# GateLoop attention and a PReLU MLP on one core: some of TensorE's waits are declared away

## The chip, the cores and the metric

The kernel runs on one NeuronCore of a Trainium2 chip. The metric is the device time of one execution in microseconds (us). Five engines work side by side, each through its own list of instructions in a fixed order: TensorE (PE in the profile: matmuls; PEld: its weight loads), VectorE (DVE), ScalarE (ACT), GpSimd (POOL) and SyncE (SP). SyncE does no arithmetic here; it issues all of the kernel's DMA transfers, one after the other. The engines meet through counters (semaphores): an instruction can be made to wait until another engine's counter, its own engine's counter or that of a DMA has reached a value.

## The reference

Two stages in float32. The first is a linear attention with a complex decay for each head and channel; the second is an MLP with a PReLU.

```python
# (batch, heads, seq, head_dim) = (4, 8, 768, 48)
mag = np.sqrt(a_re * a_re + a_im * a_im)
scale = np.minimum(mag, 0.999) / (mag + 1e-06)
a_re_n, a_im_n = (a_re * scale, a_im * scale)
for t in range(S):
    ar, ai = (a_re_n[:, :, t, :, None], a_im_n[:, :, t, :, None])
    new_re = ar * S_re - ai * S_im
    new_im = ar * S_im + ai * S_re
    kv = np.einsum('bhd,bhe->bhde', k[:, :, t], v[:, :, t])
    S_re, S_im = (new_re + kv, new_im)
    y[:, :, t] = np.einsum('bhd,bhde->bhe', q[:, :, t], S_re)
...
x = y.transpose(0, 2, 1, 3).reshape(3072, 384)
h = x @ w_in                                    # 384 -> 2048
g = np.maximum(h, 0.0) + alpha * np.minimum(h, 0.0)
return g @ w_out                                # 2048 -> 384
```

## The kernel before

The recurrence over 768 tokens is cut into 24 units: 4 batches by 6 chunks of 128 tokens (`unit(u)`). Before them, the `gates` tasks turn the gates into phases (`phs` in DRAM) and products of magnitudes (`decs` in DRAM) for several chunks at a time.

One unit works like this, with the names that the profile uses. SyncE loads `KQ` (queries and keys, three buffers), `PP` (phases, one buffer), `T` (products of decays, two buffers), `V` (values, **one** buffer) and `VL` (values laid out for six levels, one buffer, in some ten small transfers). VectorE multiplies `KQ` by the phases (L661, L663). Then come six levels h = 1, 2, 4, 8, 16, 32, taken two at a time in three visits. For a level, VectorE multiplies `KQ` by decays (L717), ScalarE copies the part that a product needs into `WQ` (L740; two slots that are handed around) or `W` (L756), TensorE multiplies keys by queries into a PSUM tile `ps_lv` (L678, two buffers), and VectorE (L702) or ScalarE (L699) masks the result into `A`. After the levels TensorE transposes the keys in two groups through one PSUM tile `ps_kt` (L785), and ScalarE copies each group into `T` (L787, L788). The product of keys and `V` goes to `ps_kv` (L797), one tile for each half (s = 0 and 1) of the chunk; VectorE decays the state `St` (L826) and adds `ps_kv` (L829), once for each half. The output `ps_y` is opened by four bf16 products (L808), gathers the products of `A` and `VL` (L817) and of `KQ` and `St` (L841), and is copied by ScalarE into `T` (L855) and sent to DRAM (`ysc`, L860).

For the MLP, `xT` is loaded back from `ysc` for one or two chunks (L873); TensorE computes `ps_h` (L889), ScalarE and VectorE make the PReLU (L896, L898), and TensorE sums `ps_o` (L908). There are 672 products on L889 and 384 on L908; in the trace a float32 product is two matmul records.

The order is written out by hand. Each task (gates, loads, units, MLP) is a Python generator; the string `ORDER` names, letter by letter, which task takes its next step. `A` to `I` are the gates, `J` the loads of `KQ`, `PP` and `T`, `K` the spreading of values in DRAM (L560), `L` the loads of `V` and `VL`, `M` to `O` the weights, `P` to `Z` and `a` to `m` the 24 units, `n` the loads of `xT`, and `o` the MLP. So the place of every instruction in its engine's list is fixed, that of every DMA in SyncE's list too. The waits are not written by hand: the framework derives them from the tiles that an instruction reads and writes. One wait can sit on the instruction itself; further ones stand ahead of it as instructions of their own (EVENT_SEMAPHORE in the trace). What is already implied by an earlier wait of the same engine is left out.

The lines around which the change turns are the loads of `V` in `loads_v` (L603, L605, L608), which are not edited:

```python
nc.sync.dma_start(V[0:P - 16], v[b, :, 1:P - 15, c].rearrange("n p e -> p n e"))       # L603
```

and the functions that are:

Of the kernel before, what the change touches and what calls it, by code (L numbers as in the profile page):

```python
# [9 lines left out]
F32 = mybir.dt.float32  # L10
# [3 lines left out]
AF = mybir.ActivationFunctionType  # L14
ALU = mybir.AluOpType
# [3 lines left out]
P = 128  # L19
# [82 lines left out]
def kernel(  # L102
# [32 lines left out]
    nc = tc.nc  # L135
    B, HP, _, D, S = q.shape
# [5 lines left out]
    D2 = 2 * D  # L142
    HC = P // 2
# [5 lines left out]
    VISITS = [(1, 2), (4, 8), (16, 32)]  # L149
    LEVELS = [h for visit in VISITS for h in visit]  # L150

    qv = q.rearrange("b n i d s -> b d (n i) s")
    kv_in = k.rearrange("b n i d s -> b d (n i) s")
# [2 lines left out]
    work = ctx.enter_context(tc.tile_pool(name="work", bufs=2))  # L156
    dram = ctx.enter_context(tc.tile_pool(name="dram", bufs=4, space=DRAM))
    ps = ctx.enter_context(tc.tile_pool(name="ps", bufs=1, space=PSUM))

    def halves(t, h):  # L160

# [3 lines left out]
    ident = consts.tile([P, P], F32, tag="ident")  # L165
# [20 lines left out]
    for h in (16, 32):  # L186
        by_row[h] = []
        for m in range(HC // h):
            t = next(column)
# [8 lines left out]
    def step(*args, **kwargs):  # L198
# [5 lines left out]
        KQ=3, PP=1, T=2, V=1, WQ=2, W=1, run=1, St=3, xT=2, raw0=1, raw1=1, raw2=1, g0=0, g1=0, g2=0, ot=2, top=2,  # L204
        lv=2, misc=1, y=1, h=2, o=1).items()}
# [255 lines left out]
    start = consts.tile([D2, B, H], F32, tag="start")  # L461
# [104 lines left out]
    def loads():  # L566
        for u in range(NU):
            b, c = divmod(u, NCH)
            cols = slice(c * P, (c + 1) * P)
            yield DMA(196, takes=(R["KQ"],))  # L570
            KQ = work.tile([D2, 2, H, P], F32, tag="KQ", name="KQ", bufs=3)
            n = min(P, S - 1 - c * P)
            if n < P:
                nc.gpsimd.memset(KQ[:, 1, :, n:P], 0.0)
            for i in range(2):
                rows = slice(i, D2, 2)
                if i:
                    yield DMA(196)
                nc.sync.dma_start(KQ[rows, 0], qv[b, :, :, cols])
                t = yield DMA(196)  # L580
                nc.sync.dma_start(KQ[rows, 1, :, 0:n], kv_in[b, :, :, c * P + 1:c * P + 1 + n])
            done["KQ", u] = t
            loaded[u] = L = dict(KQ=KQ)
            t = yield DMA(393, ("PP", u), takes=(R["PP"],))
            scr, phs, at = scr_of[u]
            L["PP"] = PP = work.tile([D2, H, P + 1], F32, tag="PP", name="PP", bufs=1)
            nc.sync.dma_start(PP, phs.rearrange("(h d) i s -> (d i) h s", d=D)[:, :, at * P:(at + 1) * P + 1])
            done["rotation", u] = t
            for i in range(2):
                rows = slice(i, D2, 2)  # L590
                t = yield DMA(393, ("T", u), takes=() if i else (R["T"],))
                if i == 0:
                    L["T"] = T = work.tile([P, H, TL], F32, tag="T", name="T", bufs=2)
                nc.sync.dma_start(T[rows], scr.rearrange("(h d) c s -> d h c s", d=D)[:, :, at])
            done["decays", u] = t

    def loads_v():
# [47 lines left out]
    def unit(u):  # L645
        b, c = divmod(u, NCH)
        r = yield DVE(H * P, ("KQ", u), ("rotation", u), takes=(R["WQ"],))
        L = loaded[u]
        KQ, PP = L["KQ"], L["PP"]
# [17 lines left out]
        def meet(h, shared, at, keys, queries, *after, takes=()):  # L667

            e = yield PE(0.28, *after, *[("met", h, u - 1)] * (u > 0), takes=takes, mode=1, n=16)
            if not shared:  # L670
                shared.append(ps.tile([P, 2, HP, HC // 2], F32, tag="lv", name="ps_lv", bufs=2))
            t = shared[0][:, at]
            for p in range(4):
                for i in range(2):
                    n = 4 * i + p
                    for g in range(2):
                        j = HC // 2 * g
                        nc.tensor.matmul(t[64 * i + j:64 * i + j + HC // 2, p], lhsT=keys(n, g),  # L678
                                         rhs=queries(n, g), start=True, stop=True)
            done["met", h, u] = e  # L680
            return e

        def mask_out(name, t, e):

            n = HC

            if name in by_row:
                e = yield ACT(HP * name + 100, e, takes=(R[name],))
            else:
                e = yield DVE(HP * n, e, takes=(R[name],))  # L690
            a = A[name] = work.tile([P, HP, n], F32, tag=f"A{name}", name=f"A{name}",
                                    bufs=2 if name <= 4 else 1)
            if name in by_row:
                for m, s in enumerate(by_row[name]):
                    if m:
                        e = yield ACT(HP * name + 100, e)
                    cols = slice(m * name, (m + 1) * name)
                    at = m * name % (HC // 2)
                    nc.scalar.activation(a[:, :, cols], t[:, :, at:at + name], AF.Copy, scale=s)  # L699
            else:  # L700
                whole = [P, HP, 2, HC // 2]
                nc.vector.tensor_tensor(out=a.rearrange("p n (g t) -> p n g t", g=2), in0=t.unsqueeze(2).to_broadcast(whole),  # L702
                                        in1=masks[name].rearrange("p (g t) -> p g t", g=2).unsqueeze(1).to_broadcast(whole),
                                        op=ALU.mult)
            made.append(e)
            return e

        def step(h, x0=None):

# [9 lines left out]
        if c == 0:  # L719
            k_ = yield DMA(144, *[("state", u - 2)] * (u > 1), takes=(R["St"],))  # L720
            St = work.tile([D2, H, D], F32, tag="St", name="St", bufs=3)
# [6 lines left out]
        for visit in VISITS:  # L728
            ready = []
            for h in visit:  # L730
                held, slot, w = None, None, k_
                if h == 1:
                    held, slot = "WQ", first_slot
                    keys, queries = [lambda n, g, z=WQ, i=i: z[:, i, n, HC // 2 * g:HC // 2 * (g + 1)] for i in (1, 0)]
                elif h != visit[-1]:
# [6 lines left out]
                    keys, queries = [lambda n, g, z=z, i=i: z[:, i, n, HC // 2 * g:HC // 2 * (g + 1)] for i in (1, 0)]  # L742
                else:
                    def queries(n, g, h=h):
                        m = HC // (2 * h)
                        return halves(KQ[:, 0, n], h)[:, :, 1][:, m * g:m * (g + 1)]

                    if h == HC // 2:
                        def keys(n, g):
                            return KQ[:, 1, n, P // 2 * g:P // 2 * g + HC // 2]  # L750
                    else:
# [6 lines left out]
                        keys = lambda n, g, W=W: W[:, n, HC // 2 * g:HC // 2 * (g + 1)]  # L758
                ready.append((h, keys, queries, held, slot, w))
                if h != visit[-1]:  # L760
                    k_ = yield DVE(2 * H * HC, w, *[("decays", u)] * (h == 1))
                    T = L["T"]
                    step(h, WQ if h == 1 else None)
            tiles, shared = [], []
# [8 lines left out]
                k_ = yield DVE(2 * H * HC, e)  # L773
                step(visit[-1])
            for h, ta, e in tiles:
                e = yield from mask_out(h, ta, e)
            R["lv"].put(e)
        q_ = k_

# [1 line left out]
        for i in range(2):  # L781
            e = yield PE(0.333, k_, takes=(R["misc"],), n=2)
            t = ps.tile([P, HP, D2], F32, tag="misc", name="ps_kt")
            for p in range(4):
                nc.tensor.transpose(t[:, p], KQ[:, 1, 4 * i + p], ident[:D2, :D2])  # L785
            e = yield ACT(HP * P + 80, e, ("decays", u))
            nc.scalar.copy(T[:, 4 * i:4 * (i + 1), 0:D2], t)  # L787
            nc.scalar.copy(T[:, 4 * i:4 * (i + 1), D2:P], t[:, :, 0:P - D2])  # L788
            R["misc"].put(e)
        e = yield PE(0.72, e, ("V", u), *[("state", u - 1)] * (u > 0), takes=(R["misc"],) if last else (R["misc"], R["lv"]), mode=2, n=16 if last else 32)  # L790
        V = L["V"]
# [1 line left out]
        for n in range(H):  # L793
            for j in range(0, P, HC):
                for s in range(1 if last else 2):
                    rows = slice(HC * s, HC * (s + 1))
                    nc.tensor.matmul(kv[s][j:j + HC, n], lhsT=T[rows, n, j:j + HC],  # L797
                                     rhs=V[rows, n // 2, (n % 2) * D:(n % 2 + 1) * D], start=True, stop=True)
        ek = e
        for s in range(2):  # L800
            for part in range(2):
# [20 lines left out]
        for s in range(1 if last else 2):  # L822
            before, known = states[s]
            k_ = yield DVE(H * D, known, takes=(R["St"],))
            St = work.tile([D2, H, D], F32, tag="St", name="St", bufs=3)
            nc.vector.tensor_tensor(out=St, in0=before, in1=T[0:D2, :, TL - 4 + s:TL - 3 + s].to_broadcast([D2, H, D]),  # L826
                                    op=ALU.mult)
            k_ = yield DVE(H * D, ek, k_)
            nc.vector.tensor_tensor(out=St, in0=St, in1=kv[s][0:D2], op=ALU.add)  # L829
            R["lv" if s else "misc"].put(k_)  # L830
            states.append((St, k_))
        if not last:
# [4 lines left out]
        for s in range(2):  # L837
            before, known = states[s]
            e = yield PE(0.47, q_, known, mode=1, n=8)
            for n in range(H):  # L840
                nc.tensor.matmul(Y[64 * (n % 2):64 * (n % 2) + D, n // 4, n // 2 % 2, HC * s:HC * (s + 1)],  # L841
                                 lhsT=before[:, n], rhs=KQ[:, 0, n, HC * s:HC * (s + 1)],
                                 start=False, stop=(s == 1 and n // 2 % 2 == 1))
            R["St"].put(e)
        R["KQ"].put(e)
        if g not in ysc_of:
# [154 lines left out]
```

## Time and profile before

| | |
|---|---|
| time before, median of 3 runs | 843.26 us (841.33 to 843.42) |
| span of the profiled execution | 845.2 us |
| TensorE busy | 699.6 us (83%) |
| VectorE busy | 653.3 us (77%) |
| ScalarE busy | 443.3 us (52%) |
| GpSimd busy | 196.3 us (23%) |
| packets of the DMA queue that SyncE feeds, as a share of 16 engines' span | 59.2% |

The profiled execution's own time is its span, 845.2 us from the first to the last instruction; it is 1.9 us (0.2%) above the median of the timed runs. In a line of the timeline the first number is the start in us from the beginning of the span, the second the length of the group, then the engine, the source line, the operation, what is written and what is read, the shape, and how many instructions are merged. Square brackets tell idle time of the engine ahead of it and what ended it. "SPq" is SyncE issuing a DMA, "PEldq" is TensorE's sequencer; a wait that is an instruction of its own is not counted as busy. The clock of TensorE that a throttle granted stands as a share of full speed.

### The profile page before, as it was taken

How to read it: one execution, taken by the hardware profiler on the slowest of the kernel's cores; microseconds unless marked ns; L12 is line 12 of the kernel's file. 1: busy time of each engine (PE TensorE's matmuls, PEld its weight loads, DVE VectorE, ACT ScalarE, POOL GpSimd, SP SyncE). 2: the span in 40 equal slices, each digit the busy share in tenths (PEclk: the TensorE clock that was granted, in tenths of full speed). 3: DMA queues.
4: the chain of work that ended last, by engine and by line, in shares of the span. 5: the costliest groups of instructions: out<-in, count | busy, mean ns of one | idle time of the engine just before them, and what ended most of it. 6: DMA issues, size and time to landing. Idle time of an engine off the chain costs nothing.

```text
span 845.2 us, 26866 instructions
## 1 busy us (share of the span) xinstructions
PE 699.6 (83%) x11488; PEld 529.6 (63%) x11488; DVE 653.3 (77%) x1020; ACT 443.3 (52%) x937; POOL 196.3 (23%) x293
## 2 busy tenths in 40 slices
PE   0002316688899999999999999999999999999998
PEld 0001315566777777767777777777676777777776
DVE  5999998689998999979998997687877656345212
ACT  7679686356745656665565634555444324233211
POOL 6241421126544411450115404300124000000000
PEclk9999997879999999999999999999999999999999
DMA  8496987675469677736965467747644482231100
GB/s 240 142 270 172 281 198 207 186 203 123 118 201 255 143 182 223 182 88 172 264 166 138 134 178 181 201 107 192 159 136 106 115 204 64 69 80 38 37 29 9
DMA packets 194174, 130.91 MB, mean 155 GB/s; under 512 B 74120, under 2 KB 185864, under 8 KB 194056
## 3 DMA queue, kind: packets, MB, share of 16 engines
q1 hardware_dynamic: 194056, 129.20, 59.2%
q8 instruction: 90, 1.47, 0.8%
q14 instruction: 28, 0.23, 0.1%
HBM read 100.82 MB, written 35.71 MB: 162 GB/s over the span
## 4 chain that ended last, share of the span: by engine, by line
PE 63%; DVE 17%; DMA 6%; issue 6%; ACT 5%; SPq 2%; POOL 0%; DVEq 0%; ACTq 0%; POOLq 0%
PE ps_o L908 25%; PE ps_h L889 25%; PE ps_lv L678 4%; DVE KQ L717 4%; PE ps_y L817 3%; PE ps_kv L797 2%; PE ps_y L841 2%; DVE gate L338 2%; DMA PP<-phs 2%; DMA phs<-gate 1%; DMA g_sb<-in_w_in_dram 1%; PE ps_kt L785 1%; DVE gate L426 1%; SPq L626 1%; DVE gate L340 1%
## 5 line engine op out<-in xcount | busy, mean ns | idle before, releaser
L889 PE MATMUL ps_h<-xT,w_in_sb 128*128 128x256 f32 (+1 forms) x1344 | 302.0, 356 | 2.9 <-DVE g_sb L898 1.6
L908 PE MATMUL ps_o<-w_out_sb,g_sb 128*128 128x384 f32 x768 | 295.2, 499 | 5.1 <-DVE g_sb L898 4.9
L889 PEld LDWEIGHTS ps_h<-xT,w_in_sb 128*128 128x128 f32 x1344 | 234.3, 193 | 74.1 <-issue 3.6
L898 DVE SCALAR_TENSOR_TENSOR g_sb<-g_sb,al,ps_h 128x256 f32<-128x256 f32 (+1 forms) x224 | 97.4, 437 | 115.5 <-ACT g_sb L896 115.1
L896 ACT ACTIVATE g_sb<-ps_h 128x256 f32<-128x256 f32 (+1 forms) x224 | 79.0, 353 | 204.2 <-PE ps_h L889 202.7
L908 PEld LDWEIGHTS ps_o<-w_out_sb,g_sb 128*128 128x128 f32 x768 | 138.0, 192 | 56.7 <-DVE g_sb L898 6.9
L717 DVE TENSOR_TENSOR KQ<-KQ,T 96x1024 f32<-96x1024 f32 x120 | 148.5, 1239 | 32.1 <-PE ps_lv L678 23.2
L678 PE MATMUL ps_lv<-WQ 96*32 96x32 f32 x2304 | 34.7, 204 | 79.0 <-DVE WQ L661 55.9
L678 PEld LDWEIGHTS ps_lv<-WQ 96*32 96x32 f32 x2304 | 26.6, 116 | 99.7 <-DVE WQ L661 56.1
L740 ACT COPY WQ<-KQ 96x1024 f32<-96x1024 f32 x48 | 50.0, 1041 | 27.8 <-DVE KQ L717 27.7
L338 POOL TENSOR_TENSOR gate<-gate 128x72 f32<-128x72 f32 x42 | 29.6, 704 | 125.6 <-ACT gate L368 122.8
L855 ACT COPY T<-ps_y 48x256 f32<-48x256 f32 x96 | 30.8, 364 | 51.8 <-PE ps_y L841 51.2
L338 DVE TENSOR_TENSOR gate<-gate 128x576 f32<-128x576 f32 (+5 forms) x84 | 50.0, 595 | 1.1
L515 POOL TENSOR_SCALAR top<-top 128x768 f32<-128x768 f32 x16 | 41.5, 2602 | 32.1 <-ACT top L507 32.1
L678 PE MATMUL ps_lv<-KQ,W 96*32 96x32 f32 x1536 | 25.2, 205 | 27.5 <-ACT W L756 23.2
L817 PE MATMUL ps_y<-A,VL 64*48 64x64 f32 x2304 | 42.4, 223 | 4.1 <-DMA VL<-vsc 2.5
L699 ACT ACTIVATE A<-ps_lv,columns 128x64 f32<-128x64 f32 x144 | 36.2, 336 | 17.2 <-PE ps_lv L678 17.1
L426 DVE TENSOR_TENSOR gate<-gate 128x1152 f32<-128x1152 f32 (+2 forms) x36 | 43.6, 1235 | 0.3
L756 ACT COPY W<-KQ 96x512 f32<-96x512 f32 x48 | 30.8, 642 | 23.9 <-DVE KQ L717 21.1
L817 PEld LDWEIGHTS ps_y<-A,VL 64*48 64x48 f32 x2304 | 39.8, 124 | 5.5 <-DMA VL<-vsc 2.7
L678 PEld LDWEIGHTS ps_lv<-KQ,W 96*32 96x32 f32 x1536 | 20.3, 115 | 29.6 <-ACT W L756 24.7
L785 PE MATMUL ps_kt<-ident,KQ 96*128 96x96 f32 x192 | 26.0, 260 | 15.4 <-DVE KQ L717 12.9
(106 smaller groups left out, 912.1 us busy)
## 6 DMA issues: line engine op xcount, KB each, us to landing
T<-decs SPq DMA_DIRECT2D x48, 384.0 KB
PP<-phs SPq DMA_DIRECT2D x24, 387.0 KB
KQ<-in_q_dram SPq DMA_DIRECT2D x48, 192.0 KB
decs<-gate SPq DMA_DIRECT2D x7, 1152.0 KB
phs<-gate SPq DMA_DIRECT2D x14, 576.0 KB
KQ<-in_k_dram SPq DMA_DIRECT2D x40, 192.0 KB
vsc<-in_v_dram SPq DMA_DIRECT2D x48, 144.0 KB
VL<-vsc SPq DMA_DIRECT2D x24, 288.0 KB
```

Source lines behind the costliest of these rows:

```text
L338: on(4 * k).tensor_tensor(out=m, in0=w[:, 1::-1].unsqueeze(2).to_broadcast([P, 2, 2, k]), in1=pairs_of(u), op=ALU.mult)
L426: TT(out=m[:, a], in0=U5[:, 1 + a], in1=turned(off3, o)[:, a].unsqueeze(1).unsqueeze(3).to_broadcast([P, L // 2, nb, 2]), op=ALU.mult)
L515: nc.gpsimd.tensor_scalar(out=top, in0=top, scalar1=F64_SMALL, scalar2=None, op0=ALU.max)
L678: nc.tensor.matmul(t[64 * i + j:64 * i + j + HC // 2, p], lhsT=keys(n, g), rhs=queries(n, g), start=True, stop=True)
L699: nc.scalar.activation(a[:, :, cols], t[:, :, at:at + name], AF.Copy, scale=s)
L717: nc.vector.tensor_tensor(out=x, in0=x if x0 is None else x0, in1=m, op=ALU.mult)
L740: nc.scalar.copy(z.rearrange("p i n t -> p i (n t)").rearrange("p i (m h) -> p m i h", h=h), bass.AP(tensor=KQ.tensor, offset=KQ.offset + ...
L817: nc.tensor.matmul(o, lhsT=Vp[h][64 * i:64 * i + 64, s, e_ * D:(e_ + 1) * D], rhs=a, start=False, stop=False)
L889: nc.tensor.matmul(p, lhsT=w_in_sb[:, f // 2, kk, f % 2 * P:(f % 2 + 1) * P], rhs=x_of[m][:, kk], start=(kk == 0), stop=(kk == NK - 1))
L896: nc.scalar.activation(gt, p, AF.Relu, scale=-1.0)
L898: nc.vector.scalar_tensor_tensor(out=gt, in0=gt, scalar=al_1[:, f:f + 1], in1=p, op0=ALU.mult, op1=ALU.add)
L908: nc.tensor.matmul(sums[0], lhsT=gt[:, c * P:(c + 1) * P], rhs=w_out_sb[:, f], start=(f == 0), stop=(f == NF - 1))
```

## The change

Three helpers are added. `of(group, i)` puts an instruction into a named group; `turned(i)` declares that an instruction need not wait for the members of the group `turned`; `read(group, i)` declares an instruction to be the fence of a group, that is, one by whose end all members of the group are done. Members of a group don't wait for one another.

- The loads into `KQ` and `T` (and the one small fill of `KQ`) become members of `turned`, and TensorE's products that read these tiles (L678, L785, L797, L841) are declared not to wait for them.
- The products of the second visit (levels 4 and 8) become members of a group `lv` of their unit, with the last mask of that visit as its fence.
- Each of the two groups of transposes (L785) becomes a group `kt`, with ScalarE's second copy (L788) as its fence.
- The products into each of the two `ps_kv` tiles (L797) become a group `kv`, with VectorE's addition to the state (L829) as its fence.

No instruction is added, removed or moved on any engine apart from the waits; tiles and buffers are the same.

```diff
+    def of(group, i):
+        tc.add_to_no_dep_group(group, i.ins)
+        return i
+    def read(group, i):
+        tc.declare_fence(i.ins, group=group)
+        return i
+    def turned(i):
+        tc.declare_no_dep(i.ins, group="turned", reason="the engine that this waits for overwrote all of it")
+        return i
...
-                nc.gpsimd.memset(KQ[:, 1, :, n:P], 0.0)
+                of("turned", nc.gpsimd.memset(KQ[:, 1, :, n:P], 0.0))
...
-                nc.sync.dma_start(KQ[rows, 0], qv[b, :, :, cols])
+                of("turned", nc.sync.dma_start(KQ[rows, 0], qv[b, :, :, cols]))
...
-                nc.sync.dma_start(KQ[rows, 1, :, 0:n], kv_in[b, :, :, c * P + 1:c * P + 1 + n])
+                of("turned", nc.sync.dma_start(KQ[rows, 1, :, 0:n], kv_in[b, :, :, c * P + 1:c * P + 1 + n]))
...
-                nc.sync.dma_start(T[rows], scr.rearrange("(h d) c s -> d h c s", d=D)[:, :, at])
+                of("turned", nc.sync.dma_start(T[rows], scr.rearrange("(h d) c s -> d h c s", d=D)[:, :, at]))
...
-                shared.append(ps.tile([P, 2, HP, HC // 2], F32, tag="lv", name="ps_lv", bufs=2))
+                shared.extend([ps.tile([P, 2, HP, HC // 2], F32, tag="lv", name="ps_lv", bufs=2), h])
...
-                        nc.tensor.matmul(t[64 * i + j:64 * i + j + HC // 2, p], lhsT=keys(n, g),
-                                         rhs=queries(n, g), start=True, stop=True)
+                        met = turned(nc.tensor.matmul(t[64 * i + j:64 * i + j + HC // 2, p], lhsT=keys(n, g),
+                                                      rhs=queries(n, g), start=True, stop=True))
+                        if shared[1] == VISITS[1][0]:
+                            of(f"lv {u}", met)
...
             for h, ta, e in tiles:
-                e = yield from mask_out(h, ta, e)
+                e, i = yield from mask_out(h, ta, e)
+            if visit == VISITS[1]:
+                read(f"lv {u}", i)
...
-                nc.tensor.transpose(t[:, p], KQ[:, 1, 4 * i + p], ident[:D2, :D2])
+                of(f"kt {u} {i}", turned(nc.tensor.transpose(t[:, p], KQ[:, 1, 4 * i + p], ident[:D2, :D2])))
...
-            nc.scalar.copy(T[:, 4 * i:4 * (i + 1), D2:P], t[:, :, 0:P - D2])
+            read(f"kt {u} {i}", nc.scalar.copy(T[:, 4 * i:4 * (i + 1), D2:P], t[:, :, 0:P - D2]))
...
-                    nc.tensor.matmul(kv[s][j:j + HC, n], lhsT=T[rows, n, j:j + HC],
-                                     rhs=V[rows, n // 2, (n % 2) * D:(n % 2 + 1) * D], start=True, stop=True)
+                    of(f"kv {u} {s}", turned(nc.tensor.matmul(
+                        kv[s][j:j + HC, n], lhsT=T[rows, n, j:j + HC],
+                        rhs=V[rows, n // 2, (n % 2) * D:(n % 2 + 1) * D], start=True, stop=True)))
...
-            nc.vector.tensor_tensor(out=St, in0=St, in1=kv[s][0:D2], op=ALU.add)
+            read(f"kv {u} {s}", nc.vector.tensor_tensor(out=St, in0=St, in1=kv[s][0:D2], op=ALU.add))
...
-                nc.tensor.matmul(Y[64 * (n % 2):64 * (n % 2) + D, n // 4, n // 2 % 2, HC * s:HC * (s + 1)],
-                                 lhsT=before[:, n], rhs=KQ[:, 0, n, HC * s:HC * (s + 1)],
-                                 start=False, stop=(s == 1 and n // 2 % 2 == 1))
+                turned(nc.tensor.matmul(Y[64 * (n % 2):64 * (n % 2) + D, n // 4, n // 2 % 2, HC * s:HC * (s + 1)],
+                                        lhsT=before[:, n], rhs=KQ[:, 0, n, HC * s:HC * (s + 1)],
+                                        start=False, stop=(s == 1 and n // 2 % 2 == 1)))
```

More of the change, by code (lines that the diff above doesn't have):

```diff
@@ L698, in mask_out @@
                     at = m * name % (HC // 2)
-                    nc.scalar.activation(a[:, :, cols], t[:, :, at:at + name], AF.Copy, scale=s)
+                    i = nc.scalar.activation(a[:, :, cols], t[:, :, at:at + name], AF.Copy, scale=s)
             else:
                 whole = [P, HP, 2, HC // 2]
-                nc.vector.tensor_tensor(out=a.rearrange("p n (g t) -> p n g t", g=2), in0=t.unsqueeze(2).to_broadcast(whole),
+                i = nc.vector.tensor_tensor(out=a.rearrange("p n (g t) -> p n g t", g=2), in0=t.unsqueeze(2).to_broadcast(whole),
                                         in1=masks[name].rearrange("p (g t) -> p g t", g=2).unsqueeze(1).to_broadcast(whole),
@@ L705, in mask_out @@
             made.append(e)
-            return e
+            return e, i
         def step(h, x0=None):
```

## The prediction

> **What bounds the kernel now.** I read the page first, then the stretches, TensorE's waits and the timeline around the loads of `V`.
>
> ```profile
> span 845.2 us, 26866 instructions
> PE 699.6 (83%) x11488; PEld 529.6 (63%) x11488; DVE 653.3 (77%) x1020; ACT 443.3 (52%) x937; POOL 196.3 (23%) x293
> PEclk9999997879999999999999999999999999999999
> ...
> 235.00:400.00 165.00, 162.62 (x2752) 123.26 (x2751) 151.90 (x204) 93.89 (x213) 55.65 (x81) 1.00 0.72 184
> 400.00:600.00 200.00, 196.90 (x3272) 147.14 (x3271) 169.28 (x228) 108.68 (x237) 43.15 (x82) 1.00 0.69 174
> ...
> PE ps_h L889 <- DVE g_sb L898: 1.6, 2, 0.8
> L797 PEldq EVENT_SEMAPHORE  x56: 51/51/1457, 82.3 to 788.5; - x56
> ```
>
> Until about 235 us TensorE has little to do; from there it is the bound (162.62 busy of 165, 196.90 of 200), and its idle time after 235 is 13.7 us in all four stretches to the end. So whatever makes TensorE wait after 235 us lengthens the kernel nearly one for one, and hardly anything is there to be gained.
>
> **The change, part by part.** The built programs have the same instructions in the same order; the waits differ.
>
> *Taken away.* Standalone waits on TensorE fall from 244 to 171. Each takes 51 ns in the sequencer (last line above). Both ends: 73 x 0.051 = 3.7 us saved, and 0. The sequencer works ahead of the array: the waits ahead of a product on L797 stand at 82 to 788 us one to four us before that product starts, and where one lasts long (up to 1457 ns, TensorE's own transposes) the product then still waits for ScalarE's copy (L788), which comes later. The cover is that copy; without it a bubble would be shorter by at most those waits. I take -0.5. TensorE also gets 35 new waits for itself, all for work 20 or more products back, over 5 us earlier: 0.
>
> *Moved, and this decides.* With the addition L829 declared the fence of the products L797, what must follow those products follows the addition instead. That holds for the next load of `V` (L603): in 21 of 24 units it waited for TensorE's L797 and now waits for VectorE's second L829. VectorE comes to that addition when its own list does: in 14 of the 21 units it ended later than the load was issued before, by 1.1 to 11.9 us, 68.6 us in all. And the load heads SyncE's one list: `VL`, `KQ`, `xT`, `PP`, `T`, `ysc` and the output stand behind it. Three places reach TensorE.
>
> ```profile
> 220.87 0.31 SPq L603 DMA_DIRECT2D V<-in_v_dram  x1
> 224.11 2.76 SPq L626 DMA_DIRECT2D VL<-in_v_dram  x3
> 226.92 0.59 SPq L873 DMA_DIRECT2D xT<-ysc  x1
> ...
> 222.65 0.54 DVE L829 TENSOR_TENSOR St<-St,ps_kv 96x384 f32<-96x384 f32 x1
> 232.19 0.54 DVE L829 TENSOR_TENSOR St<-St,ps_kv 96x384 f32<-96x384 f32 x1
> ...
> 235.95 1.46 PE L889 MATMUL ps_h<-xT,w_in_sb 128*128 128x256 f32 x6
> ```
>
> First: the addition ends at 232.73, so `V` goes from 220.87 to about 232.8, +11.9. SyncE idled 1.6 us (222.51 to 224.11) ahead of the `VL` loads, so `xT` is issued 11.9 - 1.6 = 10.3 later, at 237.2. Its last semaphore count came 4.95 us after its issue (the trace's semaphore record; `PP`, as large, took 5.8, from 582.26 to the product at 588.05 that waited for it). It lands at 242.2 and TensorE wanted it at 235.95: +6.2. SyncE's two long issues of small loads (1.28 and 1.44 us, others of their kind 0.5 to 0.6) may shrink when they come late: 4.6 is the low end, 7.0 the high one (additions late by 0.8 themselves). I take 6.2.
>
> ```profile
> 364.75 0.32 SPq L603 DMA_DIRECT2D V<-in_v_dram  x1
> 377.70 0.44 SPq L629 DMA_DIRECT2D VL<-vsc  x1
> ...
> 372.56 0.55 DVE L829 TENSOR_TENSOR St<-St,ps_kv 96x384 f32<-96x384 f32 x1
> 384.85 1.61 PE L817 MATMUL ps_y<-A,VL 64*48 64x64 f32 x96
> ```
>
> Second: +8.4, less 1.0 of SyncE's idle time on the way: `VL` is issued 7.4 later. It landed 4.2 us before the product that reads that part of it (semaphore record): +3.2, or 1.3 if two long issues shrink. Both load and product shift by the first stall, so this comes on top. I take 3.
>
> ```profile
> 650.86 0.31 SPq L603 DMA_DIRECT2D V<-in_v_dram  x1
> 661.92 0.81 SPq L629 DMA_DIRECT2D VL<-vsc  x1
> ...
> 661.70 0.54 DVE L829 TENSOR_TENSOR St<-St,ps_kv 96x384 f32<-96x384 f32 x1
> 674.84 1.53 PE L817 MATMUL ps_y<-A,VL 64*48 64x64 f32 x96
> ```
>
> Third: +11.4, less 0.7; 9.0 us of slack: +1.7 (0 to 1.7). Loads with 1 to 2 us of slack (`VL` at 447.6, `xT` at 324.0) add 1 (0 to 2). In the other units the slack covers the delay.
>
> *Added elsewhere.* Six copies `WQ` (L740) now wait for the last mask of the second visit (L702), 0.6 to 1.7 us later than they ran, 5.4 in all: +1.5, since TensorE waited for what follows in about half (0 to 5.4). VectorE gets 13 waits for itself on L717: an instruction that waits for its neighbour starts 0.03 us after its end, one that doesn't 0.08 before it (medians of the trace): 13 x 0.11 = 1.5 at most; +0.5, since VectorE is not the bound after 235. [...] ScalarE's copies on L855 wait for L829 too, in 33 places, 32 of them long done, one 0.3 us late at 95 us where TensorE idles: 0.
>
> *Given back.* TensorE's waits after 235 for engines that were not behind it: -2 (0 to -4).
>
> Sum: -0.5 + 6.2 + 3 + 1.7 + 1 + 1.5 + 0.5 - 2 = 11.4. Against its own execution that is 845.2 to 856.6 of span; against the median, 843.26 + 11.4 = 854.7.
>
> **Rivals.**
>
> (a) *The loads are hidden.* If SyncE catches up (short issues, shorter landings), the first stall shrinks to 1 or 2 and the others vanish, with ScalarE's 1.5 given back: 843.3 to 845.8. For it: most of the 14 delays die in slack. Against: 4.1 us of slack against 10.3. Somewhat less catching up gives 846 to 850.
>
> (b) *Faster.* One mechanism: TensorE's waits for its own transposes (L797, to 1457 ns) and for loads keep its sequencer from running ahead, and products after them start late. It decides if the copy L788 ends before those waits do. All idle time after 235 that could go is 13.7; the named wait on L797 would give a third of it: 838.5. Against it: what ended the waits there is ScalarE's copy, 7.6 us in 13 cases on that line's weight loads.
>
> (c) *The stall slows the clock too.*
>
> ```profile
> 170.07 1.65 PE L908 MATMUL ps_o<-w_out_sb,g_sb 128*128 128x384 f32 x2 [4.29 <-DVE g_sb L898]
> 169.30:176.00 6.70, 5.93 (x42) 4.60 (x43) 5.42 (x11) 3.69 (x5) 4.67 (x3) 0.50 1.03 294
> ```
>
> An idle stretch of 4.29 us stands ahead of 6.7 us at a granted clock of 0.50; two such products took 1.65 there and 0.91 at 189.5. After 190 the clock stayed at 1.00. A stall of 6.2 us at 236 may bring 3.4 to 10.2 us (the shortest and longest such stretch between 138 and 190) at half clock: 1.7 to 5.1 more, 856.4 to 860. [...]
>
> (d) *It doesn't do what it says*: the waits leave TensorE but its times stay, and the new waits on VectorE are met. Then 843.3, counted with (a).
>
> **How the numbers follow.** 0.3% (2.5 us) is about what a measurement of this kernel can tell from no change. Forecast, 850 to 856.4: 0.50. Clock as well: 0.18. Partly caught up, 846 to 850: 0.16. Hidden, within 0.3%: 0.09. Faster: 0.07. So slower 0.84, same 0.09, faster 0.07. The range leaves out the faster case and half of the hidden one below, 844.5; above, all high ends together (7.0 + 3.2 + 1.7 + 2 + 1.5 + 1.5 = 16.9, with 3 of clock) give 863.
>
> **What would show it.** The loads of `V` right behind L829 in SyncE's list; a wait of TensorE for `xT<-ysc` near 236 of 4.6 to 7 us, and for `VL<-vsc` near 391 and 686; the slice of the clock behind the first one. Wrong if no wait for `xT` appears there, or if TensorE's idle time after 235 falls below 13.7 us.

## The result, and the profile after

The changed kernel takes 862.02 us (median of 4 runs, 860.59 to 871.23); the kernel before took 842.48 us beside it (841.33 to 843.42). The medians lie 19.5 us apart, a quotient of 1.0232; the ratio that is estimated from all runs of both kernels is 1.0262, 95% interval 1.0216 to 1.0308. The profiled execution of the changed kernel is its fastest, 860.59 us, of which the span is 858.9 us. Between the two profiled executions the span grew by 13.7 us.

The head of the page after:

```profile
span 858.9 us, 26799 instructions
PE 704.3 (82%) x11488; PEld 532.6 (62%) x11488; DVE 654.0 (76%) x1020; ACT 442.3 (52%) x937; POOL 188.9 (22%) x293
```

The stretches behind 235 us (length, then busy us and instructions of TensorE, its weight loads, VectorE, ScalarE and GpSimd, then granted clock, DMA share, GB/s):

```profile
235.00:400.00 165.00, 154.40 (x2646) 116.32 (x2636) 143.80 (x196) 86.38 (x200) 51.57 (x83) 0.98 0.66 170
400.00:600.00 200.00, 195.10 (x3171) 145.70 (x3161) 169.46 (x227) 109.33 (x236) 44.85 (x81) 0.99 0.67 174
600.00:860.00 260.00, 253.48 (x3389) 189.90 (x3387) 135.08 (x214) 85.97 (x230) 17.86 (x39) 1.00 0.36 92
```

TensorE is busy 602.98 us after 235 us, so its idle time there is 858.9 - 235 - 602.98 = 20.9 us, 7.2 more than before. In both executions 3.5 us of the idle time lie behind TensorE's last product. Its busy time over the whole span grew by 4.7 us with the same instructions, and in the first 235 us it was busy for 1.8 us less. 7.2 + 4.7 + 1.8 = 13.7.

What ended TensorE's idle time after 236 us (us in all, times, longest), and what SyncE waited for ahead of the load of `V`, which is L618 now:

```profile
PE ps_y L837 <- DMA VL<-vsc: 5.6, 3, 2.3
PE ps_h L909 <- DMA xT<-ysc: 4.5, 2, 3.8
PE ps_lv L693 <- ACT W L773: 2.9, 3, 1.1
PE ps_y L837 <- issue: 2.0, 4, 1.0
...
SPq L618 <- DVE St L849: 82.4, 13, 15.8
SPq L618 <- DVE g_sb L918: 17.0, 3, 15.2
```

Neither of the first two stood in the list of before. SyncE's wait ahead of L603 was 34.7 us for TensorE; ahead of L618 it is 82.4 us for the addition L849 (L829 before). The 15.2 us that the last line puts down to `g_sb` are the wait ahead of 235.04 us, which the timeline shows to end with the addition too. Of the 24 loads of `V`, 15 are issued 0.03 us after an addition ends. The first place behind 235 us in the timeline after:

```profile
234.47 0.54 DVE L849 TENSOR_TENSOR St<-St,ps_kv 96x384 f32<-96x384 f32 x1
235.04 0.31 SPq L618 DMA_DIRECT2D V<-in_v_dram  x1
236.12 2.11 SPq L641 DMA_DIRECT2D VL<-in_v_dram  x3
238.27 0.60 SPq L893 DMA_DIRECT2D xT<-ysc  x1
...
242.17 2.93 PE L909 MATMUL ps_h<-xT,w_in_sb 128*128 128x256 f32 x6 [3.79 <-DMA xT<-ysc]
```

The load of `V` is issued 0.03 us after the second addition ends, `xT` stands behind it, and TensorE waits 3.79 us for it. Just ahead of this wait the same instructions ran 2.4 us later than before, from here on 6.2. Three further places, at each of which the last load of `VL` comes too late:

```profile
384.75 0.32 SPq L618 DMA_DIRECT2D V<-in_v_dram  x1
395.94 0.47 SPq L644 DMA_DIRECT2D VL<-vsc  x1
399.18 1.34 PE L837 MATMUL ps_y<-A,VL 64*48 64x64 f32 x80 [2.31 <-DMA VL<-vsc]
...
468.64 1.34 PE L837 MATMUL ps_y<-A,VL 64*48 64x64 f32 x80 [1.88 <-DMA VL<-vsc]
...
690.00 1.33 PE L837 MATMUL ps_y<-A,VL 64*48 64x64 f32 x80 [1.44 <-DMA VL<-vsc]
```

And the clock, in the stretches right behind the first wait and behind the one at 468 us (TensorE's busy time first, granted clock third from the end):

```profile
241.20:248.10 6.90, 5.93 (x74) 4.11 (x74) 1.75 (x2) 0.87 (x2) 0.46 (x2) 0.51 0.62 153
469.90:473.30 3.40, 3.40 (x43) 2.99 (x37) 2.05 (x2) 1.36 (x5) 0.00 (x0) 0.51 0.30 65
```

Before, the clock was not halved between 190 us and the last slice of the span. The shift of the same product against before, by the times of the changed kernel, reads 2.4 us at 238, 6.2 at 242, 7.9 at 246, 13.7 at 328, 14.1 at 399, 16.7 at 468, 18.2 at 473, 15.2 at 655, 13.2 at 668.4, 14.9 at 690 and 13.7 at the end.

### The profile page after: what moved, and what is told of

Same layout as the page of the kernel before. It is cut to its first block, busy times and chain, and to the rows that moved or that the text cites. A ratio compares the mean times of both kernels' runs of the same rounds, so it can differ in the third digit from the quotient of the medians.

```text
span 858.9 us, 26799 instructions
## 1 busy us (share of the span) xinstructions
PE 704.3 (82%) x11488; PEld 532.6 (62%) x11488; DVE 654.0 (76%) x1020; ACT 442.3 (52%) x937; POOL 188.9 (22%) x293
## 4 chain that ended last, share of the span: by engine, by line
PE 54%; DVE 17%; DMA 11%; issue 6%; SPq 6%; ACT 4%; POOL 1%; DVEq 0%; ACTq 0%; POOLq 0%
PE ps_o L928 21%; PE ps_h L909 21%; PE ps_lv L693 4%; SPq L641 3%; DVE KQ L734 3%; PE ps_y L837 3%; DMA T<-decs 2%; PE ps_y L861 2%; PE ps_kv L816 2%; DVE gate L353 2%; DMA xT<-ysc 2%; DMA g_sb<-in_w_in_dram 1%; DVE gate L441 1%; DVE gate L355 1%; PE ps_kt L804 1%
## 5 line engine op out<-in xcount | busy, mean ns | idle before, releaser
L353 POOL TENSOR_TENSOR gate<-gate 128x72 f32<-128x72 f32 x42 | 26.2, 625 | 139.6 <-ACT gate L383 136.8
L837 PE MATMUL ps_y<-A,VL 64*48 64x64 f32 x2304 | 44.5, 225 | 12.3 <-DMA VL<-vsc 7.1
L837 PEld LDWEIGHTS ps_y<-A,VL 64*48 64x48 f32 x2304 | 40.9, 126 | 14.9 <-DMA VL<-vsc 7.7
L773 ACT COPY W<-KQ 96x512 f32<-96x512 f32 x48 | 30.7, 640 | 27.0 <-DVE KQ L734 25.3
L804 PEld LDWEIGHTS ps_kt<-ident,KQ 96*128 96x128 f32 x192 | 21.5, 148 | 24.6 <-issue 9.9
```

The costliest lines, as they stand in the source:

```text
L353: on(4 * k).tensor_tensor(out=m, in0=w[:, 1::-1].unsqueeze(2).to_broadcast([P, 2, 2, k]), in1=pairs_of(u), op=ALU.mult)
L804: of(f"kt {u} {i}", turned(nc.tensor.transpose(t[:, p], KQ[:, 1, 4 * i + p], ident[:D2, :D2])))
L837: nc.tensor.matmul(o, lhsT=Vp[h][64 * i:64 * i + 64, s, e_ * D:(e_ + 1) * D], rhs=a, start=False, stop=False)
```

## The experiments

Each run stands beside the kernel before on the same chip, so ratios are compared, and times only where they were taken together.

**The group kv left out.** Of the changed kernel, only the group of L816 and its fence go.

```diff
-                    of(f"kv {u} {s}", turned(nc.tensor.matmul(
+                    turned(nc.tensor.matmul(
...
-            read(f"kv {u} {s}", nc.vector.tensor_tensor(out=St, in0=St, in1=kv[s][0:D2], op=ALU.add))
+            nc.vector.tensor_tensor(out=St, in0=St, in1=kv[s][0:D2], op=ALU.add)
```

> The changed kernel without the group kv and its fence; everything else of the change stays, so the loads of V wait for TensorE's products again. Theory (the load of V, behind the second addition of VectorE, holds up SyncE's one list): almost all of the loss goes, 842 to 846 us, no wait of TensorE for xT near 236. Rival (the missing waits of TensorE or the new waits of ScalarE's copies WQ for the last mask cost the time): still above 855 us.

Measured: 840.67 us, ratio 0.9917 (0.9879 to 0.9955). The whole loss is gone and a gain stands in its place. No wait for `xT` is left after 236 us, and 0.8 us for `VL`.

**The group kv alone**, put into the kernel before.

```diff
-                    nc.tensor.matmul(kv[s][j:j + HC, n], lhsT=T[rows, n, j:j + HC],
+                    of(f"kv {u} {s}", nc.tensor.matmul(kv[s][j:j + HC, n], lhsT=T[rows, n, j:j + HC],
...
-            nc.vector.tensor_tensor(out=St, in0=St, in1=kv[s][0:D2], op=ALU.add)
+            read(f"kv {u} {s}", nc.vector.tensor_tensor(out=St, in0=St, in1=kv[s][0:D2], op=ALU.add))
```

> The kernel before with the group kv and its fence alone; TensorE keeps its waits for loads and the other groups are not made. Theory: nearly the whole loss comes with this part, 856 to 863 us, with TensorE's waits for xT near 242 and for VL near 399 and 690. Rival (the parts that take waits off TensorE or add them to ScalarE and VectorE): 842 to 847 us.

Measured: 869.89 us, ratio 1.0275 (1.0232 to 1.0318), with TensorE's waits in the same two places:

```profile
PE ps_y L827 <- DMA VL<-vsc: 5.0, 3, 2.5
...
PE ps_h L899 <- DMA xT<-ysc: 3.9, 2, 3.6
```

This one pair of declarations is the loss: its ratio is that of the whole change (1.0262) within the intervals. The time lies above the 856 to 863 us that were expected, beside a kernel before that took 847.07 us here and 842.48 us beside the changed kernel.

**The group kv for the first half only**, so that the load of `V` follows the first addition and TensorE's products of the second half.

```diff
+                    if s == 0:
+                        of(f"kv {u} {s}", met)
...
+            if s == 0:
+                read(f"kv {u} {s}", i)
```

> The changed kernel with the group kv for the first half's tile alone: the load of V then waits for TensorE's last product and for the first of the two additions, which stood at 222.65 where the second stood at 232.19, at 364.93 instead of 372.56 and at 651.52 instead of 661.70. Theory (the lateness of the second addition is the price): V is late by about 2.3, 0.7 and 1.2 us at these places, SyncE's idle time takes most of that, 843 to 848 us. Rival (any wait of the loads for VectorE costs the same, since VectorE is busy): 856 us or more.

Measured: 845.01 us, ratio 0.9991 (0.9955 to 1.0026). It is the second addition, the later one, that hurts.

**The load of `xT` ahead of `V`.** One letter of `ORDER` moves: the step that loads `xT` near 236 us comes before the steps of `V`.

```diff
-    "ooTLJooDTTToooDUUTTTTTToULLLLULEEEEooEoTEoEDDDDDDDDDoDDEooooooUEToooUUUoooooonoUoEooJoUoooooUEUEDTDD"
+    "ooTLJooDTTToooDUUTTTTTToUnLLLLULEEEEooEoTEoEDDDDDDDDDoDDEooooooUEToooUUUoooooooUoEooJoUoooooUEUEDTDD"
```

> The changed kernel with one load of xT, the one for the first two-chunk group, moved ahead of the load of V in SyncE's list; no wait is changed otherwise. Theory (head of the line: xT was late because it stood behind V, not for its own sake): the wait near 242 (3.8 us of idle time, 6.2 us of delay) and the 6.8 us at half clock after it go, about 8 us less than the changed kernel, 852 to 857 us; the waits for VL near 399 and 690 stay. Rival (the delay would come anyway, from VectorE, since the additions are on the path): within 2 us of the changed kernel.

Measured: 863.22 us, ratio 1.020 (1.0143 to 1.0257), beside a kernel before of 847.07 us. That can't be told from the ratio of the changed kernel, where 8 us less were expected. The gain came where it was expected: at 242 us TensorE stood 0.4 us ahead of the changed kernel, where it had been 3.8 us behind at 210. It was lost again: 2.3 us behind at 276, 5.4 at 336. One reloaded tile was taken out of the queue behind `V`; the others still stood there (`VL<-vsc` waits of 3.5 us), and the clock was halved at 275, 329 and 405 us instead.

**The changed kernel again**, beside the next three.

> The changed kernel once more, beside the three that follow. Theory: 858 to 867 (ratio about 1.02 to 1.03 to the kernel before). The profile must again show TensorE waiting for `xT<-ysc` near 240 us for 3 to 4 us and for `VL<-vsc` at two or three places after 390 us. Rival: part of what was put down to these waits was the spread of single executions; then the waits come at other places, or the time lies under 852.

Measured: 865.68 us, ratio 1.0232 (1.0194 to 1.0270), with `xT` waits of 5.7 us (longest 3.9) and `VL` waits of 3.9 us. The place and size repeat.

**All of the change, with the loads of `V` issued behind those of `VL`.** The loads of `V` keep their wait for VectorE, and in the source only their place in SyncE's list moves. TensorE's list moves with it: it has 36 fewer standalone waits (173 of them in the trace of the changed kernel, 137 here).

```diff
-            L["V"] = V = work.tile([P, HP, D2], F32, tag="V", name="V", bufs=1)
-            nc.sync.dma_start(V[0:P - 16], v[b, :, 1:P - 15, c].rearrange("n p e -> p n e"))
             yield DMA(24)
...
             nc.sync.dma_start(VL[:, k:k + len(SPREAD)].rearrange("p l n e -> p l (n e)"),
                               vsc_of.pop(u).rearrange("l i t e -> (i t) l e"))
+            L["V"] = V = work.tile([P, HP, D2], F32, tag="V", name="V", bufs=1)
+            nc.sync.dma_start(V[0:P - 16], v[b, :, 1:P - 15, c].rearrange("n p e -> p n e"))
```

> All of the change stays, the loads of V still wait for VectorE's second addition, but they are issued behind the loads of VL of the same unit instead of ahead of them, so that neither VL nor the xT load at 236 us stands behind them. Theory (the cost is what is queued behind the waiting load in SyncE's list): no wait of TensorE for VL<-vsc over 1 us after 236 us, none for xT there, and 838 to 848, near what the change costs without the group kv. Rival one (the late V itself is what hurts): TensorE waits for V ahead of its products of keys and V, and the time stays at 855 to 865. Rival two (the load that stood ahead of V only passes the delay on, as the run with xT ahead showed): the waits move to PP, T or ysc, which still stand behind V, and the time is 850 to 860.

Measured: 859.49 us, ratio 1.0156 (1.0124 to 1.0187). The waits for `xT` and `VL` are gone, as the theory had it, but the time hardly fell. What TensorE waited for after 236 us:

```profile
PE ps_y L838 <- issue: 11.3, 6, 3.0
PE ps_lv L694 <- issue: 2.7, 1, 2.7
PE ps_kv L817 <- DMA V<-in_v_dram: 1.5, 1, 1.5
```

At the product that the kernel before runs at 369 us it was 4.1 us ahead of that kernel, at the one of 710 us 14.0 behind. One of the places between, in the timeline:

```profile
447.15 0.38 SPq L640 DMA_DIRECT2D VL<-vsc  x1
...
452.11 0.99 PE L838 MATMUL ps_y<-A,VL 64*48 64x64 f32 x54
456.07 1.33 PE L838 MATMUL ps_y<-A,VL 64*48 64x64 f32 x41 [2.97 <-issue]
```

A stop of 2.97 us in the middle of 96 products, all with their operands present: `VL`'s last semaphore count had come at 450.17 us. Neither of the two rivals put on record fits. What does is the number of the instruction. Counted through TensorE's list (from 0, each product is two entries, its weight load and its matmul, and each standalone wait is one; a stop is given the number of the weight load), the stops of this run over 0.9 us that end in "issue" stand at

```
start us   idle us   number   number mod 256   packet of the instruction queue (16,384 bytes), start to end
416.50      2.71     10944        192          416.66 to 417.69
453.10      2.97     11968        192          453.39 to 454.64
570.56      1.52     15809        193          569.26 to 570.70
593.21      2.72     16576        192          593.19 to 594.40
683.98      2.87     19392        192          684.31 to 685.27
721.56      0.94     20416        192          720.20 to 721.12
```

Over all 14 traces of this case TensorE has 84 idle stretches of 0.9 us or more after 235 us. 47 of them stand at a number that leaves 192 or 193, where chance would put one in 128; each of the other 37 ended with a load (`xT`, `VL`, `V`) or with work of ScalarE or VectorE. All 47 stops end between 1.24 and 1.64 us after the end of a packet of 16,384 bytes. The page of the profile lists the queue that moves these packets:

```profile
q8 instruction: 90, 1.47, 0.7%
```

An estimate from these figures: if a packet holds 256 entries, as the period says, 90 packets are 23,040 entries, about the length of TensorE's list (23,116 here). So TensorE seems to run out of its own instructions where 256 of them pass faster than the next packet comes, which is in the runs of short products (96 on `A` and `VL`, 192 entries, pass in about 1.5 us). What a packet holds no trace shows. The idle time at these numbers is 14.0 us in this run. Around three of the stops the clock was halved, for 6.8 us at 455.8 and at 595.7, and for 3.4 at 687.9.

**The change without the group lv.**

```diff
-                        if shared[1] == VISITS[1][0]:
-                            of(f"lv {u}", met)
...
-            if visit == VISITS[1]:
-                read(f"lv {u}", i)
```

> The change without the group lv: the copies WQ need not wait for the last mask of the second visit. Prediction's term for it: 1.5 us (0 to 5.4) less than the changed kernel, so 857 to 861 if that one is at 860 to 862. Rival (these waits make VectorE late, which makes the addition and the loads behind it later still): 4 to 8 us less, 853 to 857. Rival (the loads decide and VectorE catches up): within 1 us of the changed kernel.

Measured: 865.44 us, ratio 1.0222 (1.0184 to 1.0260), 0.24 us from the changed kernel beside it. A cost of the waits of the copies `WQ` can't be told from none; both intervals are some 3 us wide to either side.

**The change without the groups kv and lv** (both edits above together).

> The change without the groups kv and lv: what stays is that TensorE's products don't wait for the loads into KQ and T, and the groups kt. Theory (both groups that were left out only add waits): 836 to 842, at or a little below the run without kv alone (0.9917 of the kernel before). Rival (the prediction's first term, waits that others cover): within 0.3% of the kernel before. The run without kv left open whether its gain of 0.8% is from TensorE's waits that went or from the clock in its own executions: with a gain here too, at the same place (before 235 us, by less time at half clock), the second stays possible; a gain of TensorE's bubbles after 235 us speaks for the first.

Measured: 839.62 us, ratio 0.9926 (0.9900 to 0.9953). The gain repeats. TensorE's idle time after 235 us is 11.0 us here and 13.7 before; of that, 3.4 and 7.1 us stand at the numbers 192 and 193.

**The same list, moved against the packets.** Products of zeros into an empty PSUM tile stand at the start of TensorE's list, where it has nothing to do for 50 us (its first product starts at 51.01 us in the kernel before). They change no result and shift the number of every later instruction. Four kernels: all of the change with `V` behind `VL` and 27 products (54 instructions); the changed kernel with 16; the kernel before with 111, and with 64 (128 instructions, half of the period of 256).

```diff
+    early = ps.tile([P, 2, 512], F32, tag="y", name="ps_y")
+    for _ in range(27):
+        nc.tensor.matmul(early[0:D, 0, 0:2 * P], lhsT=nothing[0:64], rhs=ident.bitcast(BF16)[0:64], start=True, stop=True)
```

> The run with V's loads behind VL's had no wait for VL or xT left after 236 us, but 13.7 us of idle time of TensorE at six places that no record of a semaphore explains. Each stands at an instruction whose number in TensorE's list leaves 192 or 193 when divided by 256, beside a packet of 16,384 bytes of the instruction queue, and three of them are followed by half clock (17.0 us in all). Here 27 products of zeros (54 instructions) stand at the start of TensorE's list, where it is idle, so that other instructions come to these numbers. Theory (TensorE waits there for its own instructions): these places go, some 2 to 4 us of such idle time are left, and the time falls by 12 to 21 us to 838 to 847, about what the change costs without the group kv. Rival (late loads of V make the stalls): 855 to 862, with the stalls at the same products.

Measured: 840.36 us, ratio 0.9979 (0.9949 to 1.0008), from 1.0156 without the 54 instructions. The idle time at those numbers fell from 14.0 to 2.4 us, the clock was not halved between 235 us and the last slice, and the run of products that had stopped at 453 us passed in one piece. TensorE's waits after 236 us:

```profile
PE ps_kv L820 <- DMA V<-in_v_dram: 2.4, 3, 1.3
PE ps_lv L697 <- issue: 1.4, 1, 1.4
PE ps_y L841 <- issue: 1.0, 2, 0.6
```

In its timeline:

```profile
453.68 1.55 PE L841 MATMUL ps_y<-A,VL 64*48 64x64 f32 x95
```

So with every declaration of the change in place the loss is gone once the loads of `V` stand behind those that TensorE needs sooner and few stops are left. The wait of `V` itself costs 2.4 us of idle time; that the time is no longer than before owes something to the stops, 2.4 us here and 7.1 in the kernel before.

> The changed kernel with 16 products of zeros (32 instructions) at the start of TensorE's list. It had 3.7 us of such idle time after 224 us (at 224, 327, 435, 582 and 667 us). Theory: it falls to 2 to 3 us and nothing else goes, so the waits for xT and VL stay and the time is 858 to 865, at most 4 us under the changed kernel. Rival (the instruction queue, and not the loads, made most of the loss): 850 or less.

Measured: 861.74 us, ratio 1.0226 (1.0181 to 1.0270). The loads' waits stay (5.8 us for `xT`, 4.9 for `VL`), and so does the time. The shift took little of the idle time at those numbers away (3.3 us are left), so this run by itself decides little; but 3.3 us here, 4.0 in the changed kernel and 7.1 in the kernel before, all after 224 us, say that the loss of the change does not come from the instruction queue.

> The kernel before with 111 products of zeros (222 instructions) at the start of TensorE's list and nothing else changed. Its 7.1 us of such idle time after 224 us should fall to 2 to 4 us. Theory (the 0.7 to 0.8% that the change gains without the group kv is this, and not the waits themselves): 838 to 843, a ratio of 0.992 to 0.997. Rival (the waits that were taken away gain it): within 0.3% of the kernel before.

Measured: 845.75 us, ratio 1.0016 (0.9981 to 1.0051). The shift missed its aim: idle time at those numbers was 8.5 us after 235 us, at seven new places, not 2 to 4. With about as much of it as before the time is the same, so the 222 instructions themselves cost nothing that can be told. Whether the gain without kv is from the waits or from the numbers stays open.

> The kernel before with 64 products of zeros (128 instructions) at the start of TensorE's list. Put half a block away, the numbers that leave 192 fall into the runs of short products of nearly every unit. Theory, from the times between those places in the trace of before: 15 to 30 us more idle time, 858 to 880, as much as the whole change costs. Rival (the packets of the instruction queue only happen to stand there): within 0.3% of the kernel before.

Measured: 873.28 us, ratio 1.0359 (1.0308 to 1.0410). Nothing differs from the kernel before but 128 instructions in an empty stretch, and it is 31 us slower, more than the change under study. All its larger waits after 236 us are of this kind:

```profile
PE ps_y L820 <- issue: 17.3, 12, 2.9
PE ps_y L844 <- issue: 9.4, 3, 3.9
PE ps_lv L681 <- issue: 3.1, 1, 3.1
```

The longest of them in the timeline:

```profile
607.52 0.81 PE L844 MATMUL ps_y<-KQ,St 96*48 96x64 f32 x21
612.25 0.88 PE L844 MATMUL ps_y<-KQ,St 96*48 96x64 f32 x11 [3.92 <-issue]
```

Sixteen places, each at 192 or 193, 29.8 us, and the clock halved behind five of them for 27 us.

## Why the prediction was right or wrong

**Right: what decides.** The load of `V` inherits the wait for VectorE's second addition (82.4 us ahead of L618) and blocks SyncE's list. The runs with kv alone, without kv, with kv for the first half, and with `V` moved behind `VL` show it from four sides.

**The step that failed: what happens ahead of 235 us was put at nothing.** The prediction had it that until about 235 us TensorE has little to do, that three places, all behind 235 us, reach it, and that in the other units the slack covers the delay. In the unit whose `V` is loaded at 135 us it does not. These lines are of the kernel before:

```profile
135.12 0.33 SPq L603 DMA_DIRECT2D V<-in_v_dram  x1
159.59 0.36 SPq L431 DMA_DIRECT2D phs<-gate  x1
167.07 0.56 DVE L517 TENSOR_SCALAR top<-top 128x768 uint32<-128x768 uint32 x1 [4.59 <-POOL gate L249]
```

and these of the changed one, in which TensorE's stop at this product, 4.29 us before, is 6.94 us:

```profile
144.18 0.33 SPq L618 DMA_DIRECT2D V<-in_v_dram  x1
160.68 1.66 SPq L446 DMA_DIRECT2D phs<-gate  x1
169.04 0.56 DVE L532 TENSOR_SCALAR top<-top 128x768 uint32<-128x768 uint32 x1 [7.23 <-POOL gate L264]
172.04 1.65 PE L928 MATMUL ps_o<-w_out_sb,g_sb 128*128 128x384 f32 x2 [6.94 <-DVE g_sb L918]
```

The stores of the phases stand behind `V` in SyncE's list as well. The last count of the last one comes at 166.27 us instead of 164.30. GpSimd's wait ahead of its next fill of `gate` (L249, L264 now) ends 0.03 us later in both; VectorE waits for what GpSimd does next, and TensorE for the PReLU that VectorE does then. In all six traces in which `V` waits for the second addition ahead of these stores, TensorE stops here for 6.6 to 9.9 us; in the other eight, for 1.8 to 4.3. The delay is not made up: between 189.8 and 235 us TensorE was busy for 40.02 of 45.20 us already before. At the product that the kernel before runs at 228 us, the six stand 2.2 to 6.6 us behind it, and the other eight lie between 4.7 us ahead of it and 1.0 behind. The means of the two sets are 6.3 us apart. As an estimate, that is what this step left out, since the kernels and chips of the 14 traces differ; the two profiled executions of before and after hold 2.2 us of it.

**Right in kind: the wait for `xT`; its size came out by luck.** It was to be issued at 237.2, land at 242.2 and cost 6.2 us, with 4.6 as the low end. It was issued at 238.27, its last count came at 242.13 and the product ran at 242.17, 6.2 us later than before. But 2.4 us of these stood there before the wait, from the place above. The wait is 3.79 us of idle time, and 3.5 to 4.3 us in the five executions that have it, under the low end. The addition was 2.3 us later than before (234.47 against 232.19), and a landing 3.86 us after the issue, not 4.95, gave part of that back.

**About right: the waits for `VL`.** 3 + 1.7 + 1 for the loads at 385, 675 and elsewhere; idle 2.31, 1.44 and 1.88 (the one at 468 us, which had been given part of 1). TensorE's own waits for loads come to 10.1 us (5.6 + 4.5) where the sum had 11.9. Missing is a path over two engines: `T` stands behind `V` too, VectorE waited for it for 1.23 and 1.58 us, and ScalarE's copies `W` (L773) behind it made TensorE wait for 1.05 us at 278 and 1.00 us at 326.

**Wrong: the clock was a rival and not a term.** Case (c) had 1.7 to 5.1 us and a chance of 0.18. It came: 6.8 and 3.4 us at half clock are, as an estimate, 5.1 us of lost work, and the busy time of the products from the one at 242 us on grew by 4.1 (595.5 to 599.6). The prediction looked at one stretch of the trace of before, behind 4.29 us of idle time. The same trace has one behind 1.75 us:

```profile
186.24 0.64 PE L678 MATMUL ps_lv<-KQ,W 96*32 96x32 f32 x32 [1.75 <-ACT W L756]
186.30:189.70 3.40, 3.40 (x41) 2.73 (x42) 3.38 (x7) 1.57 (x3) 0.00 (x0) 0.50 1.00 242
```

So half clock behind the 1.88 us at 468 us could have been expected. The trace doesn't tell what counted besides the length of the idle time: behind the 2.31 us at 399 us the granted clock stayed at 1.00.

**Not told apart: the copies `WQ`.** Taken at 1.5 us (0 to 5.4); the run without lv has 0.24, with some 3 us to either side.

**Wrong in size: the waits taken away.** Taken at -0.5 (0 to -3.7). Without kv and lv the kernel gains 0.74%, 6.2 us of 845.06 (4.0 to 8.5), more than rival (b)'s 4.8, and perhaps for another reason: in the profiled executions 7.1 - 3.4 = 3.7 us is less idle time at the numbers 192 and 193. The prediction priced a removed wait by its 51 ns and by what it covers, not by what its absence does to the numbers of all instructions behind it. That these 3.7 us explain the gain is not shown: the run with 222 instructions, which was to test it, missed its aim.

**Given back: near in size, by another cause.** The sum had -2 for TensorE's waits for engines that were not behind it; 4.5 us came back between 473 us and the end (18.2 to 13.7). Of the 13.7 us of idle time after 235 us that the kernel before has, 7.1 are stops at the list numbers. The changed kernel has 2.8, since fewer waits stand in its list and other instructions come to these numbers. In the stretch that gave time back the kernel before has three stops of more than 0.9 us, 4.5 us in all at 538, 655 and 756 us, and the changed one has one, 1.03 us at 583. So the change was given 4.3 us by the places of its instructions, which nothing in the prediction foresaw.

**Wrong: the base.** For the two profiled executions the account is 2.4 us ahead of the wait for `xT`, 10.1 for loads, 4.1 for the clock, 1.4 of other idle time, and 4.3 less at the list numbers: 13.7, where the terms had 11.4. The remaining 5.8 us to the 19.5 between medians lie in the step "against the median, 843.26 + 11.4". The span was taken for the execution's own time. About 2.0 us lie around a span of the kernel before (847.04 against 845.0 in a later run), so that execution took some 847.2 us, 4.7 above the median of 842.48, while the one profiled after is the fastest of its four, 1.4 below its median. Part of the 4.7 us can be the stop near 170 us: it lasts 4.29 us in that execution, at the upper end of the eight traces without the late `V`, and 1.76 us in both traces of the same kernel with products of zeros. The repeated run's profiled execution, with a span of 866.4 us, is as much as 7.5 above the first; 4.4 of these stand there already at 230 us.

## What to carry to other kernels

When a dependence is handed on to a later instruction (a fence), ask which later writers of the same buffers now wait for that instruction's engine, and what stands behind them in their queue; here one transfer that waited at the head of SyncE's shared list made TensorE wait for those behind it, 4.5 us for `xT` and 5.6 for `VL`. Moving it behind the urgent ones took these waits away (a ratio of 1.0156), and the time came back once the stops of the new list were moved as well (0.9979). Follow what stands behind it over more than one engine, and from the start of the kernel: the stretch ahead of 235 us, in which TensorE is not yet the bound, left a delay that is estimated above at 6.3 us. Where an engine runs long stretches of very short instructions, look at idle time that names no releaser and at its place in the list: here 128 more instructions at the start of the list cost 31 us, where the change under study cost 19.5. So compare variants with their idle time at these places taken apart.

## What the runs showed of the hardware that was not expected

- TensorE stopped at list numbers that leave 192 or 193 mod 256, for up to 3.92 us at one place, and went on 1.24 to 1.64 us after the end of a packet of the instruction queue (q8); 128 instructions more at the start cost 31 us (873.28 against 842.50), 54 more saved 1.8% in another kernel (a ratio of 0.9979 against 1.0156).
- Every idle stretch of TensorE of 0.9 us or more after 235 us that is shown as "issue", in all 14 traces, was of this kind (47 of them).
- Half clock for 3.4 us followed idle stretches of 1.75 us (at 186 us, before) and 1.88 us (at 468 us, after), while the waits of 2.31 us at 399 us and 1.44 at 690 us were followed by none.
